# Expert slots worked on between pieces of later sequences' attention, with a slot table per sequence

## Chip, cores and metric

One core of a Trainium2 chip. The metric is the device time of one execution in microseconds (us); the kernel before takes 1216.33 us (median of 3 runs, 1215.55 to 1217.69).

## What is computed

```python
# q, k, v: (8 sequences, 8 heads, 576 positions, 64), float32
mask_plain = (rel >= 0) & (rel < 32)                             # heads 0-3
mask_dil   = (rel >= 0) & (rel < 128) & (rel % 4 == 0)           # heads 4-7
attn = softmax(where(mask, q @ k.T / 8, -1e9));  x = attn @ v    # x: (4608, 512)
expert_idx = argmax(x @ w_gate)                                  # 8 experts
y[tokens of e] = relu(x[tokens of e] @ w1[e]) @ w2[e]            # 512 -> 1024 -> 512
out = gate_w[:, None] * y                # gate_w: softmax weight of the chosen expert
```

Everything is float32. Which tokens an expert gets is known only when the router has run.

## The kernel before

**Attention.** The loop at L408 goes over 8 sequences b. A sequence has 8 units: type `ty` (0 sliding heads, 1 dilated heads), head pair `hl`, half of the queries `g`. `turn` (L173) turns q and k of two heads on PE, once for the two units of a pair. `front` (L220) is one unit's softmax: scores S on PE (L230), scale and mask on DVE (L242), a minimum on DVE (L252), six or eight exponentials on ACT that also sum (L255), `den` and `rec` on DVE (L263, L265), and the product with `rec` on POOL (L266). `back` (L271) turns the weights W on PE (L278), copies them out of PSUM as eT (L143), multiplies by v (X on PE, L292) and copies the result into xT (L145). `settle` lets a unit's `back` come two units after its `front`.

**Routing.** Behind each sequence's last unit `route` (L308) turns x back into rows (L314), computes logits (L324), each token's expert, gate and place among its expert's tokens (about 30 small DVE operations, L345 to L392, and the `rank` matmuls), and scatters the 576 rows into the experts' buckets in DRAM (six indirect DMAs on POOL, L113).

**Slots.** When all sequences are routed, a table (L435 to L505) gives each of 43 slots of 128 rows an expert, in the order of the experts, after eight scatters of blank rows that fill up the last slots of the experts. `fetch` (L512) loads a slot's rows x and, where its weight set still holds another expert's, w1 and w2 of 2 MB each; there are two sets, taken in turn. `slot` (L524) turns x (4 transposes), makes ph with w1 (32 matmuls, L537), takes the rectified h out of PSUM on ACT (first half, L545) and DVE (second half, L547), makes py with w2 (8 matmuls of 512 columns, L550), scales it on ACT (L552) and scatters it to the output on POOL (L555). One trace record is half of a matmul and a whole transpose.

**Order.** In this kernel the order of each engine's instructions is chosen by a scheduler, which moves instructions of different units past each other. The attention's pools are closed before the slots' pools are opened: PSUM is 3 buffers of two banks (`big`: scores, turned, weights) and 2 of one bank (`one`) in the attention. All loads of q, k, v, x and weights are issued from SP's queue, one behind the other.

Of the kernel before, what the change touches and what calls it, by code (L numbers as in the profile page):

```python
# [10 lines left out]
F32 = mybir.dt.float32  # L11
# [12 lines left out]
# Tokens go to the router in tiles of 96; six of them are one sequence.  # L24
TT, NT = 96, S // 96
# Each expert has a bucket of rows in DRAM that holds every token if need be; the experts' tokens
# are then worked on in slots of 128 rows, of which no routing needs more than NSLOT.
# [4 lines left out]
NOWHERE = 1.0e6  # L32


def _constants():
    """Masks, identity and index tables, side by side; all follow from the shapes."""
    i, j = np.arange(96)[:, None], np.arange(128)[None]

    def band(rel):
# [15 lines left out]
        "edge": np.tile(128 * np.arange(N // 128), (128, 1)),  # L55
        "row": p[:, None],
        "upto": np.tile((e[None] <= e[:, None]).reshape(1, -1), (128, 1)),
        "slot": np.tile(np.arange(NSLOT), (128, 1)),
    }
    at, k, cols = {}, 0, []  # L60
# [10 lines left out]
def kernel(  # L71
# [13 lines left out]

    cpool = ctx.enter_context(tc.tile_pool(name="cpool", bufs=1))
    cst = cpool.tile([128, packed.shape[1]], F32, name="cst")
# [7 lines left out]
    nc.vector.memset(blank[:, DM + 1 : ROW], NOWHERE)  # L95

# [7 lines left out]
    def wrote_bucket(i):  # L104
        """The writes to the buckets are to different rows: none waits for another."""
        i = getattr(i, "ins", i)
        tc.declare_no_dep(i, group="bucket", reason="no row is written twice")
        tc.add_to_no_dep_group("bucket", i)
        bucket_writes.append(i)

    def to_bucket(idx, rows):
        wrote_bucket(
            nc.gpsimd.indirect_dma_start(  # L113
                out=bucket,
                out_offset=bass.IndirectOffsetOnAxis(ap=idx, axis=0),
                in_=rows,
                in_offset=None,
                bounds_check=NROWS - 1,
                oob_is_err=False,
            )  # L120
        )

    # Unused slots read these rows.
    wrote_bucket(nc.sync.dma_start(bucket[E * CAP : NROWS], blank))

    # ---------------------------------------------------------------- attention
    attn = ExitStack()
    pool = attn.enter_context(tc.tile_pool(name="apool", bufs=2))
    big = attn.enter_context(tc.tile_pool(name="psbig", bufs=3, space=PSUM))
    one = attn.enter_context(tc.tile_pool(name="psone", bufs=2, space=PSUM))  # L130
# [16 lines left out]
    def load(b):  # L147
        """Heads 0-3 slide: q and k with a token in each partition of six tiles. Heads 4-7 are
        dilated: q and k with eight tokens in a row of a partition. v has the keys of each block of
        queries on the partitions."""  # L150
        t = {}
        for name, src in (("q", q), ("k", k)):
            x = t[name, 0] = pool.tile([TT, NT, 4, DH], F32, tag=name + "0", name=f"{name}0_{b}")
            for h in range(4):
                nc.sync.dma_start(x[:, :, h, :], src[b, h].rearrange("(t p) d -> p t d", p=TT))
        x = t["v", 0] = pool.tile([128, 4, NT, DH], F32, tag="v0", name=f"v0_{b}")
        nc.sync.dma_start(x[:, :, 0, :], v[b, 0:4, 0:128, :].rearrange("h p d -> p h d"))
        for h in range(4):
            a = v[b, h, 64:192, :]
            nc.sync.dma_start(  # L160
                x[:, h, 1:NT, :],
                bass.AP(a.tensor, a.offset, [[DH, 128], [TT * DH, NT - 1], [1, DH]]),
            )
        for name, src in (("q", q), ("k", k)):
            x = t[name, 1] = pool.tile([72, 4, 512], F32, tag=name + "1", name=f"{name}1_{b}")
            nc.sync.dma_start(x, src[b, 4:8].rearrange("h (p x) d -> p h (x d)", p=72))
        x = t["v", 1] = pool.tile([128, 4, 2, DIL * DH], F32, tag="v1", name=f"v1_{b}")
        for g in range(2):
            a = v[b, 4:8, 64 * g : 64 * g + 512, :]
            nc.sync.dma_start(x[:, :, g, :], a.rearrange("h (p r) d -> p h (r d)", r=DIL))  # L170
        return t

    def turn(t, ty, hl):  # L173
        """q and k of two heads, turned. Sliding: (head, dim) on the partitions, positions in order.
        Dilated: (residue's parity, dim) on the partitions, and head, the residue's other bit, and
        the residue's positions in order."""
        got = []
        for name in "qk":
            src = t[name, ty]
            dst = pool.tile([128, S], F32, tag=name + "T", name=name + "T", bufs=3)  # L180
            ps = bank2("turned")
            if ty == 0:
                for i in range(NT):
                    nc.tensor.transpose(
                        ps[:, i // 3, TT * (i % 3) : TT * (i % 3) + TT],
                        src[:, i, 2 * hl : 2 * hl + 2, :].rearrange("p h d -> p (h d)"),
                        ident[0:TT, 0:TT],
                    )
                evac(dst.rearrange("p (a t) -> p a t", a=2), ps[:, :, 0:288])
            else:  # L190
                for h in range(2):
                    for m in range(4):
                        nc.tensor.transpose(
                            ps[:, h, 72 * m : 72 * m + 72],
                            src[:, 2 * hl + h, 128 * m : 128 * m + 128],
                            ident[0:72, 0:72],
                        )
                    evac(
                        dst.rearrange("p (h m t a) -> p h a m t", h=2, m=2, a=2)[:, h],
                        ps[:, h, 0:288].rearrange("p (a m t) -> p a m t", a=2, m=2),  # L200
                    )
            got.append(dst)
        return got

    def blocks(ty, g):
        """The blocks of one half of the queries, by the half of the partitions that they are on:
        first query and first key in the turned q and k, head, and place among the half's."""
# [12 lines left out]
    def front(qT, kT, ty, g):  # L220
        """Softmax weights of two heads, queries on the partitions."""
# [19 lines left out]
        e = pool.tile([nq, 2, w], F32, tag=f"e{ty}", name="e", bufs=3)  # L241
# [29 lines left out]
    def back(ev, t, xT, ty, hl, g):  # L271
        """The weighted sum of v, with (head, dim) on the partitions and the tokens in order."""
        nq, bl = (96, 72)[ty], blocks(ty, g)
        nb = len(bl[0])
# [7 lines left out]
        evac(eT, tp[:, :, 0:288])  # L282
        xo = bank("xo")
        vt = t["v", ty]
# [23 lines left out]
    def route(b, xT):  # L308
        """Each token's expert, gate and row, and its x, gate and number to its expert's bucket."""
        rows = []  # L310
        for i in range(NT):
# [5 lines left out]
            row = pool.tile([TT, ROW], F32, tag="row", name="row", bufs=8)  # L317
            evac(row[:, 0:DM], ps[0:TT])
            rows.append(row)
        ps = bank("logits")  # L320
        lg = ps[0:TT, 0 : NT * E].rearrange("p (t e) -> p t e", e=E)
        for i in range(NT):
            for c in range(4):
# [6 lines left out]
                )  # L330
        shape = [TT, NT, E]
# [15 lines left out]
        # The first of equal logits has the largest of E - e.  # L347
# [5 lines left out]
        nc.vector.tensor_reduce(out=gate, in_=dl, axis=AX, op=OP.add)  # L353
        nc.vector.tensor_scalar(gate, gate, 1e-9, None, op0=OP.add)
        nc.vector.reciprocal(gate, gate)

        # How many tokens before this one have its expert: those of its tile, of the tiles before
        # it, and of the sequences before it.
# [4 lines left out]
        nc.vector.tensor_copy(counts, before[:, NT])  # L363
        ps = bank("rank")
# [14 lines left out]
        )  # L379
        pick, dest, idx = small("pick", NT, E), small("dest", NT), small("idx", NT, dt=I32)  # L380
# [9 lines left out]
        for i in range(NT):  # L390
# [8 lines left out]
            to_bucket(idx[:, i : i + 1], rows[i])  # L399

    waiting = []

    def settle(n):
        while len(waiting) > n:
            waiting.pop(0)()

    loaded = [load(0)]
    for b in range(B):  # L408
        t = loaded[b]
        xT = pool.tile([128, 4, S], F32, tag="xT", name=f"xT_{b}")  # L410
        for ty in range(2):
            for hl in range(2):
                qT, kT = turn(t, ty, hl)
                for g in range(2):
                    ev = front(qT, kT, ty, g)
                    settle(1)
                    waiting.append(
                        lambda ev=ev, t=t, xT=xT, ty=ty, hl=hl, g=g: back(ev, t, xT, ty, hl, g)
                    )
            if ty == 0 and b + 1 < B:  # L420
                loaded.append(load(b + 1))
# [179 lines left out]
```

## Time and profile before

| | us |
|---|---|
| median of 3 runs | 1216.33 |
| span of the profiled execution (first to last instruction) | 1191.1 |
| time of the runs less that span | 25.2 |
| PE busy in the span | 1036.2 (87%) |
| DVE, ACT, POOL busy | 328.2, 294.6, 201.8 |
| first score matmul | 13.54 |
| last scatter of routed rows begins | 513.6 |
| first ph matmul, last py matmul's end | 541.86, 1180.1 |

The profile gives busy time per engine, the clock that TensorE was granted (1.00 is full), and for stretches of the span the same numbers apart. A busy PE is a PE with a matmul in flight; at half clock it is as busy as at full clock and does less.

### The profile page before, as it was taken

Reading aid. Unit: us, or ns where it says so; the run is one execution under the profiler, and the core shown is the slowest. Engines: PE = TensorE matmul, PEld = TensorE weight load, DVE = VectorE, ACT = ScalarE, POOL = GpSimd, SP = SyncE. Lnnn points to the kernel's source line nnn. Section 1 sums busy time; section 2 is a strip of 40 time slices with the busy share of each in tenths; the row PEclk is TensorE's granted clock in tenths of the full one; section 3 lists DMA queues with packets and bytes.
Section 4 is the critical chain, followed back from the end, with each engine's and each line's share of the span. In section 5 each row is a group of like instructions: output and inputs, shape, how many; then the busy total and the mean of one; then the engine's idle time right before and its main releaser. Section 6 shows DMA issues by size and latency. Waiting matters only on the chain.

```text
span 1191.1 us, 17878 instructions
## 1 busy us (share of the span) xinstructions
PE 1036.2 (87%) x6910; PEld 796.0 (67%) x6910; DVE 328.2 (28%) x812; ACT 294.6 (25%) x1127; POOL 201.8 (17%) x167
## 2 busy tenths in 40 slices
PE   5797979788888888608999999999999999999996
PEld 4586857676767676506677777777777777777774
DVE  4555454545454645410100000101001011000000
ACT  3535354544445454300000000000000000000000
POOL 1314141424242424140000000000000000000000
PEclk9666676666667676658999999999999999999998
DMA  9934343434341101028172824545145451811100
GB/s 218 213 79 107 76 107 76 107 77 106 77 106 37 41 1 41 1 83 310 36 274 76 280 73 145 207 147 206 36 161 185 169 183 36 311 36 36 34 9 1
DMA packets 115684, 134.18 MB, mean 113 GB/s; under 512 B 67662, under 2 KB 75854, under 8 KB 115472
## 3 DMA queue, kind: packets, MB, share of 16 engines
q1 hardware_dynamic: 107776, 112.26, 32.3%
q0 software_dynamic: 7152, 19.71, 4.9%
q10 hardware_dynamic: 672, 1.07, 0.3%
q8 instruction: 55, 0.90, 0.3%
q14 instruction: 29, 0.24, 0.1%
HBM read 226.29 MB, written 23.11 MB: 209 GB/s over the span
## 4 chain that ended last, share of the span: by engine, by line
issue 51%; POOL 4%; POOLq 0%
POOL out_dram L555 3%; POOL bucket L113 0%; POOLq L555 0%; POOLq L597 0%
## 5 line engine op out<-in xcount | busy, mean ns | idle before, releaser
L537 PEld LDWEIGHTS ph<-xt,w 128*128 128x128 f32 x2752 | 314.9, 193 | 28.3 <-issue 14.6
L537 PE MATMUL ph<-xt,w 128*128 128x128 f32 x2752 | 319.3, 277 | 13.1 <-DVE xt L529 6.6
L550 PE MATMUL py<-w,h 128*128 128x512 f32 x688 | 302.4, 592 | 0.0
L550 PEld LDWEIGHTS py<-w,h 128*128 128x128 f32 x688 | 127.4, 190 | 144.0 <-issue 143.2
L255 ACT ACTIVATE e<-e,lo 72x128 f32<-72x128 f32 (+1 forms) x448 | 172.7, 388 | 33.2 <-DVE lo L252 21.2
L266 POOL TENSOR_TENSOR e<-e,rec 96x768 f32<-96x768 f32 (+1 forms) x64 | 107.6, 1681 | 330.3 <-DVE rec L265 303.9
L230 PE MATMUL scores<-kT,qT 64*72 64x128 f32 (+1 forms) x896 | 127.7, 417 | 35.8 <-ACT kT L145 35.8
L555 POOL DMA_INDIRECT out_dram<-y,to x43 | 41.8, 971 | 609.4 <-ACT y L552 609.4
L547 DVE TENSOR_SCALAR h<-ph 128x512 f32<-128x512 f32 x43 | 29.8, 692 | 411.4 <-issue 298.9
L552 ACT ACTIVATE y<-py,x 128x512 f32<-128x512 f32 x43 | 29.5, 687 | 421.2 <-PE py L550 421.2
L230 PEld LDWEIGHTS scores<-kT,qT 64*72 64x72 f32 (+1 forms) x896 | 92.1, 235 | 52.3 <-ACT kT L145 37.6
L278 PE MATMUL weights<-cst,e 72*128 72x72 f32 (+1 forms) x448 | 75.5, 329 | 24.9 <-ACT qT L145 17.6
L292 PE MATMUL xo<-eT,v 128*64 128x72 f32 (+1 forms) x896 | 82.1, 314 | 16.0 <-DVE idx L389 10.5
L242 DVE SCALAR_TENSOR_TENSOR e<-scores,cst 96x768 f32<-96x768 f32 (+1 forms) x64 | 69.4, 1084 | 84.3 <-PE scores L230 84.3
L292 PEld LDWEIGHTS xo<-eT,v 128*64 128x64 f32 x896 | 68.7, 195 | 28.7 <-issue 17.1
L278 PEld LDWEIGHTS weights<-cst,e 72*128 72x128 f32 (+1 forms) x448 | 56.5, 203 | 45.8 <-issue 30.4
L255 ACT ACTIVATION_READ_ACCUMULATOR e<-e,lo 72x1 f32 (+1 forms) x448 | 84.5, 189 | 0.0
L545 ACT ACTIVATE h<-ph 128x512 f32<-128x512 f32 x43 | 25.7, 597 | 200.1 <-PE ph L537 200.1
L145 ACT COPY xT<-xo 128x288 f32<-128x288 f32 x64 | 33.8, 528 | 164.5 <-PE xo L292 164.5
L252 DVE TENSOR_REDUCE lo<-e 96x6 f32<-96x768 f32 (+1 forms) x64 | 68.4, 1069 | 0.3
L529 DVE COPY xt<-xt 128x512 f32<-128x512 f32 x43 | 27.9, 687 | 122.5 <-PE xt L527 122.5
L143 DVE COPY eT<-weights 128x576 f32<-128x576 f32 x64 | 48.0, 749 | 16.3 <-PE weights L278 16.0
(82 smaller groups left out, 536.2 us busy)
## 6 DMA issues: line engine op xcount, KB each, us to landing
w<-in_moe_w_dram SPq DMA_DIRECT2D x86, 2048.0 KB
x<-bucket SPq DMA_DIRECT2D x43, 257.0 KB
v<-in_v_dram SPq DMA_DIRECT2D x16, 512.0 KB
v<-in_v_dram SPq DMA_DIRECT2D x32, 160.0 KB
q<-in_q_dram SPq DMA_DIRECT2D x32, 144.0 KB
k<-in_k_dram SPq DMA_DIRECT2D x32, 144.0 KB
q<-in_q_dram SPq DMA_DIRECT2D x8, 576.0 KB
k<-in_k_dram SPq DMA_DIRECT2D x8, 576.0 KB
```

What stands on the lines that cost most here:

```text
L143: nc.vector.tensor_copy(dst, src)
L145: nc.scalar.copy(dst, src)
L230: nc.tensor.matmul(sc[0:nq, r, 128 * n : 128 * n + 128], lhsT=qT[rows, q0 : q0 + nq], rhs=kT[rows, k0 : k0 + 128], start=True, stop=True,)
L242: nc.vector.scalar_tensor_tensor(out=e, in0=sc[0:nq, :, 0:w], scalar=-SCALE, in1=m.unsqueeze(1).broadcast_to([nq, 2, w]), op0=OP.mult, op1 ...
L252: nc.vector.tensor_reduce(out=lo, in_=ev, axis=AX, op=OP.min)
L255: nc.scalar.activation(out=ev[:, n], in_=ev[:, n], func=AF.Exp, bias=lo[:, n : n + 1], scale=-1.0, accum_out=den[:, n : n + 1],)
L266: nc.gpsimd.tensor_tensor(out=ev, in0=ev, in1=rec.unsqueeze(2).broadcast_to([nq, 2 * nb, 128]), op=OP.mult)
L278: nc.tensor.transpose(tp[:, r, nq * n : nq * n + nq], ev[:, nb * r + n], ident[0:nq, 0:nq])
L292: nc.tensor.matmul(xo[DH * h : DH * h + DH, nq * i : nq * i + nq], lhsT=vv, rhs=eT[:, r, nq * n : nq * n + nq], start=True, stop=True,)
L537: nc.tensor.matmul(ph[:, fi], lhsT=w1[:, c, 128 * f : 128 * f + 128], rhs=xt[:, c], start=c == 0, stop=c == 3,)
L550: nc.tensor.matmul(py, lhsT=h[:, f], rhs=w2[:, f], start=f == 0, stop=f == 7)
L555: i = nc.gpsimd.indirect_dma_start(out=out, out_offset=bass.IndirectOffsetOnAxis(ap=to, axis=0), in_=y, in_offset=None, bounds_check=N - 1 ...
```

## The change

Each expert's slots that are sure to be full need not wait for the last sequence. After b sequences at least (576 b - 8*127)/128 slots are full whatever the routing; the table of one such stage is made behind each sequence's routing from the second on, and its slots are worked on between pieces of the later sequences' attention. The stages end at slots 2, 6, 11, 15, 20, 24 and 43.

- `manual_schedule`: every engine runs its instructions in the order in which they are written, not in one that a scheduler chose.
- `attention` is a generator. It writes a unit's scores and softmax up to the product on POOL, then the W and, after the turns, the X of the unit two before, and gives a cost (1.2, 0.8, 0.7, 0.9) at each piece. q, k and v tiles have one buffer instead of two; PSUM is 2 two-bank buffers and 1 one-bank buffer for the attention, 2 for ph and 1 shared by py and the turned x.
- `moe` writes the slots as a generator too, 4 matmuls of ph (0.93) or 1 of py (0.88) a piece; the turned x of the next slot comes in the middle of a slot; a scatter is written in the next slot.
- The loop at the end writes, for each unit of attention cost, `rate` units of slots, where `rate` is what is left of the known slots over 42.
- The table has one more step: a stage takes the experts' free full slots in an order that is rotated by stage, and deals them to the two weight sets; the last stage is dealt in the same way. `fetch` gives x, w1 and w2 separately, as soon as the buffer's last reader is written.

```diff
+READY = [max(0, -(-(S * (b + 1) - E * 127) // 128)) for b in range(B)]
+READY[B - 1] = NSLOT
+LAG = 2
...
+    ctx.enter_context(tc.manual_schedule())
+    big = ctx.enter_context(tc.tile_pool(name="psbig", bufs=2, space=PSUM))
+    one = ctx.enter_context(tc.tile_pool(name="psone", bufs=1, space=PSUM))
+    psh = ctx.enter_context(tc.tile_pool(name="psh", bufs=2, space=PSUM))
+    psy = ctx.enter_context(tc.tile_pool(name="psy", bufs=1, space=PSUM))
...
+    def attention():
+        for i in range(len(units) + LAG):
+            if i < len(units):
+                evs[i] = front(qT["q"], qT["k"], ty, g)
+                yield 1.2, None
+            if i >= LAG:
+                eT = weights(evs.pop(i - LAG), ...)
+                yield 0.8, None
+            if i + 1 < len(units) and g == 1:
+                for n in "qk":
+                    qT[n] = turn(b2, ty2, hl2, n)
+                    yield 0.7, None
+            if i >= LAG:
+                summed(eT, b2, xTs[b2], ty2, hl2, g2)
+                yield 0.9, (b2, xTs.pop(b2)) if last else None
...
+    wanted = []
+    for j in range(NSLOT):
+        wanted += [(j, "x", 0, j - 2), (j, "w1", 0, j - 1), (j, "w2", 1, j - 1)]
...
+    def run_slots(limit):
+        while clock["owed"] > 0:
...
+            c = next(slots)
+            clock["moe"] += c
+            clock["all"] += c
+            clock["owed"] -= c
...
+                    clock["ready"].append((clock["all"] + 14.0, j1))
+                    left = SLOT * j1 - clock["moe"]
+                    clock["rate"] = left / 42.0
+    for cost, ended in attention():
+        clock["all"] += cost
+        clock["owed"] += cost * clock["rate"] / 2
+        run_slots(1e9)
+        if ended:
...
+            routing.append((ended[0], route(*ended, use)))
+        run_routing()
+        clock["owed"] += cost * clock["rate"] / 2
+        run_slots(1e9)
```

`front` itself is unchanged in text; `route` yields after each row tile, in the middle of the logits and before `rank`, and each yield is followed by attention and slot pieces.

## Prediction

> **What bounds it now.** I read the share of busy time and the granted clock over the span first, then stretches of the span, then the timelines of one attention unit and of one pair of slots, then the waits.
>
> From the profile page, the 40 slices of about 30 us:
>
> ```profile
> PE   5797979788888888608999999999999999999996
> PEclk9666676666667676658999999999999999999998
> ```
>
> Three stages: 17 slices of attention with PE at 0.7 to 0.9 and the clock near 0.67, a hole, and slots with PE full at clock 1.0. The same stages, as stretches (us; busy time and instructions of PE, PEld, DVE, ACT, POOL; clock; DMA share; GB/s):
>
> ```profile
> 212.00:274.00 62.00, 51.04 (x424) 42.54 (x424) 33.03 (x85) 30.55 (x135) 19.68 (x15) 0.67 0.38 88
> 264.00:268.00 4.00, 4.00 (x23) 3.13 (x23) 3.77 (x20) 1.61 (x9) 0.00 (x0) 0.50 0.00 0
> 493.00:541.90 48.90, 12.62 (x97) 10.24 (x96) 11.29 (x60) 2.66 (x5) 13.35 (x14) 0.57 0.29 98
> 541.90:558.00 16.10, 16.10 (x79) 12.75 (x80) 0.84 (x2) 0.60 (x1) 0.00 (x0) 0.82 1.03 393
> 558.00:1150.00 592.00, 583.84 (x3361) 424.57 (x3361) 57.34 (x121) 51.37 (x80) 38.86 (x40) 1.00 0.39 134
> ```
>
> A sequence costs 62 us, 51 of them with PE busy at 0.67; last routing, table and first loads leave PE idle for 36 of 48.9 us; 592 us of slots lose 8. So 11 us a sequence, 36 us of the hole, and the slow clock under the attention are all there is to win. Two slots on PE:
>
> ```profile
> 707.73 1.04 PE L527 MATMUL xt<-cst,x 128*128 128x128 f32 x8
> 709.12 7.41 PE L537 MATMUL ph<-xt,w 128*128 128x128 f32 x64 [0.35 <-DVE xt L529]
> 716.36 7.03 PE L550 MATMUL py<-w,h 128*128 128x512 f32 x16
> 723.23 7.31 PE L537 MATMUL ph<-xt,w 128*128 128x128 f32 x64
> 730.38 7.03 PE L550 MATMUL py<-w,h 128*128 128x512 f32 x16
> 737.25 1.04 PE L527 MATMUL xt<-cst,x 128*128 128x128 f32 x8
> ```
>
> From start to start two slots take 29.52 us, 14.76 each: 7.22 ph (0.226 a matmul), 6.87 py (0.859), 0.52 of transposes, the rest a wait that the change removes. So 14.61 is a slot.
>
> **The written order.** The built order of the changed kernel has on DVE, for every unit, L242, L252, den, rec, and only then the eT copy of the unit two before. den needs the last exponential, and PE's X needs eT, and the next S stands behind X. So a unit has a chain in which nothing overlaps. Its links, from a stretch where nothing else is in the way:
>
> ```profile
> 13.54 2.88 PE L230 MATMUL scores<-kT,qT 64*96 64x128 f32 x24 [0.73 <-ACT kT L145]
> ...
> 15.18 0.95 DVE L242 SCALAR_TENSOR_TENSOR e<-scores,cst 96x768 f32<-96x768 f32 x1 [4.06 <-PE scores L230]
> ...
> 16.17 0.95 DVE L252 TENSOR_REDUCE lo<-e 96x6 f32<-96x768 f32 x1
> ...
> 17.15 0.40 ACT L255 ACTIVATE e<-e,lo 96x128 f32<-96x128 f32 x1 [3.67 <-DVE lo L252]
> ...
> 19.60 0.17 DVE L263 TENSOR_SCALAR den<-den 96x6 f32<-96x6 f32 x1
> 19.80 0.19 DVE L265 RECIPROCAL rec<-den 96x6 f32<-96x6 f32 x1
> ```
>
> From 15.18 to rec's end at 19.99 is 4.81; with 0.08 ahead, the eT copy (0.76) and 0.08 of hops, C = 5.73 us from S to X for a sliding unit. A dilated one has 1.22 and 1.20 on DVE and eight exponentials 0.385 apart: C = 7.08. Now the scheduler puts other units' work into that gap; DVE waits little for it (62 us from 212; total, times, longest):
>
> ```profile
> DVE den L263 <- ACT e L255: 6.9, 5, 2.7
> ```
>
> After the change it waits 2.4 or 3.2 us in each of 8 units.
>
> **Sequences 0 to 2, without slots.** A unit costs S + C + X, plus one turn (its second PSUM buffer comes free only with eT) where g is 1. At half clock, start to start: S 1.53 or 1.90, X 1.13 or 1.65, turn 1.0 or 0.9. Units: 8.4 and 9.4 sliding, 10.6 and 11.5 dilated, 10.1 and 11.0 where the type changes. Sequence 0: the first two, which have no X, 12.0, then 8.4 + 9.4 + 10.1 + 11.0 + 10.6 + 11.5 = 73. Sequences 1 and 2 carry routing: row transposes behind X 1.1 in two units; the unit with logits has 9.9 instead of C, then 3.4 of waits for `rank` and the row operations: 88.6. Sequence 2 also has a table, 24 small DVE operations between rec and eT; rows of the present table (0.09 to 0.2 each, two of 0.45) give 4.3. From 13.5 the first S of sequence 3 starts at 268 if all is at half clock, 257 if a third is at full as now. I take 265; three sequences cost now 186.
>
> **Sequences 3 to 7, with slots.** Counting PE's built order, 19.2 of the 43 slots lie ahead of the last S. A unit costs S + max(C, what PE has between S and X) + X + what PE has behind X. At full clock: S 0.80 or 1.04, W 0.55 or 0.58, X 0.60 or 0.90, turn 0.52, row tile 0.50, logits 0.196 a matmul. Example, sequence 4's last two units: (1) 12 ph 2.71 + W 0.58 + 2 py 1.72 = 5.01, under C: 1.04 + 7.08 + 0.90 + 3 py 2.58 = 11.60, PE idle for 2.1. (2) 3 py, W, 8 ph, turn, 8 ph, turn, transposes, 4 ph = 9.22: 1.04 + 9.22 + 0.90 + 8 ph 1.80 = 12.97, not idle. So every other unit hides C, the others lose 0 to 3 us. The sequences: 82.9, 95.7, 99.4, 100.0 and 87.5 (seven units) = 465.5. On top, per sequence: table 4.3; `rank` and row operations 2.5; one PSUM bank for row tiles and X, so that two copies behind ACT or DVE stand ahead of X, 2.5; the slots' DVE copies (0.69) ahead of eT, 2.3: 11.6, five times 58. Sequence 3 has slots in 37 of its 83 us only; 8 for half clock there.
>
> **Tail.** PE's order from the last S: 364, nearly all slots, with the last routing between them. From `tot` to the first slot of the last stage are 34 us of slots. Needed: six row scatters and eight blank ones at 1.22 and 1.28 a step, 17.6, about 4 to land, then x and w1: 2 MB at 393 GB/s is 5.3; about 30. So the hole goes; 4 for waits. Behind the last py 11, as now (1180.1 to 1191.1).
>
> **Loads.** Run on the reference's inputs, the table has 16 loads of a weight pair before and 30 after: 59 MB more. A pair is 4.19 MB, 10.7 us at 393 GB/s. Each is asked for 22 us of slots ahead of use, and between attention a slot lasts some 25 us. A sequence has 4.3 slots, at most 46 us of weights and about 23 of other DMA (0.38 of 62) in 110: hidden, cost 0; if the cover fails, up to 10.7 a load. The constants are 0.3 MB more on ACT's queue; they land at 6.6, with q needed at 9.1: 0, else 1. POOL's and SP's issues keep their number apart from loads; a scatter of 0.97 ahead of a product has two units of slack.
>
> **Sum.** 265 + 465.5 + 58 + 8 + 364 + 4 + 11 = 1175.5 against 1191.1, 15.6 less. The runs' median lies 25.2 above the span: **1200.7 us**. The change wins 282 us of slots under attention and 40 of the hole, and pays them back in longer attention. The unknowns: the added waits, 58, lie between 10 (all but the table's under slots) and 130 (each of 19 slots held 4 us more by h or y behind the exponentials); the clock.
>
> The row at 264 has PE busy all of 4 us at 0.50, while slots get 1.00 within 16 us (0.82 there); so attention's matmuls alone do not raise the clock, slots do, and mixed ones are some 60% slots. I take full clock there. The Trainium skill, "TensorE: Matmul & The Clock Gate", "Why this matters for your kernels", says to avoid idle gaps over about 3 us. By that, sequences 0 to 2 (gaps of 5 us in each unit) stay at half throughout, 3 us more than I take, and the mixed ones stay full; its rule that 4 us of continuous work gives full clock is not what the row at 264 shows.
>
> **Rivals.**
> - *Waits stack up* (slower): DVE and ACT, held by den and the exponentials, also hold the slots' h, turned x and y, so PE idles in pieces that I count as full. For it: each stands behind them in the built order. Against: most are read half a slot later. At 130 instead of 58: **1273**; it decides from 16 us of extra idle.
> - *The clock drops* in mixed sequences to 0.8 on average: 92 us of PE work a sequence becomes 115, some of it in idle time: 20 in each of 4.4: **1289**. For it: attention's 0.67; against: slots' 1.00.
> - *Weight loads are late*, 2 us for each of 20 loads between attention: **1241**. For: single SP queue; against: 22 us of lead.
> - *Waits hide* (faster): 10 instead of 58, and 257 for the first stage: **1145**.
> - That slots do not move is excluded by the built order.
>
> **Chances.** Sum as worked, 1180 to 1225: 0.50. Waits stack up: 0.15. Clock: 0.10. Loads: 0.07. Waits hide: 0.18. The range 1143 to 1272 leaves out half of the clock and stacking cases and part of the last. A measurement tells 0.2% (2.4 us) from no change. Faster: 0.37 of the first and the last, 0.55; same 0.05; slower 0.40.
>
> **What would show it.** Each step: about 85 us between first scores of sequences 0 to 2; waits of den for the exponentials over 150 us in total; about 110 us per mixed sequence with PE over 85% and clock over 0.95; the last stage's first slot without a gap; ph's waits for weights near 0. Wrong if PE idles over 20 us in a mixed sequence or its clock is under 0.9.

## Result and the profile after

The changed kernel takes 1252.84 us (median of 4 runs, 1251.94 to 1253.76), the kernel before beside it 1215.94 (4 runs, 1214.11 to 1217.69): a ratio of 1.030, 95% interval 1.028 to 1.032. It is slower by 37 us, where 1200.7 was forecast; the profiled execution has a span of 1251.5 us at a mean clock of 0.859.

The slices of the changed kernel's page, about 31 us each:

```profile
PE   3546656546768896998789699977979999999996
...
PEclk8566556567689968999889999989988999999999
```

The hole ahead of the slots is gone and the clock is up from a third of the span on, as the change means it. But the attention now reaches to slice 28, with PE at 0.3 to 0.6 for the first nine. Stretches of the changed kernel: sequences 0 and 2, 3 to 7 (the last without its last unit), tail (the columns as before):

```profile
14.80:89.00 74.20, 36.97 (x288) 30.03 (x286) 27.09 (x44) 27.98 (x124) 13.43 (x8) 0.59 0.31 73
182.00:279.00 97.00, 53.35 (x410) 45.30 (x406) 39.43 (x107) 30.54 (x129) 19.00 (x14) 0.59 0.46 146
279.00:402.00 123.00, 89.37 (x650) 68.81 (x650) 43.66 (x115) 34.84 (x136) 21.21 (x16) 0.79 0.40 125
402.00:529.00 127.00, 105.99 (x750) 79.73 (x750) 46.13 (x119) 36.25 (x138) 23.05 (x18) 0.85 0.59 192
529.00:649.00 120.00, 103.67 (x772) 76.87 (x771) 45.68 (x120) 35.93 (x138) 23.00 (x18) 0.94 0.47 151
649.00:765.00 116.00, 100.18 (x790) 76.83 (x790) 45.29 (x120) 37.15 (x140) 24.04 (x19) 0.97 0.68 220
765.00:867.00 102.00, 89.42 (x698) 67.76 (x697) 40.88 (x113) 31.79 (x120) 20.11 (x16) 0.97 0.51 171
867.00:1251.00 384.00, 361.10 (x2151) 266.71 (x2146) 52.05 (x147) 37.88 (x71) 39.72 (x40) 0.98 0.49 166
```

The mixed sequences take 102 to 127 us and leave PE idle for 13 to 34 us in each. The two waits that name the cause, on VectorE and on TensorE (total, times, longest):

```profile
DVE den L303 <- ACT e L295: 182.7, 62, 3.6
```

```profile
PE xo L337 <- DVE eT L178: 60.5, 12, 10.8
PE turned L234 <- ACT qT L180: 32.5, 16, 4.4
```

`den` waited five times, 6.9 us in all, in the old stretch of 62 us; it now waits for the exponentials in 62 of the 64 units, 2.9 us each. TensorE's 60.5 us are only the waits that end with `eT` itself. One unit of sequence 1 in the changed kernel's timeline (start, duration, instruction, and idle time before it with its releaser):

```profile
88.02 1.19 PE L270 MATMUL scores<-kT,qT 64*96 64x128 f32 x12
...
89.14 0.72 PE L317 MATMUL weights<-cst,e 72*128 72x72 f32 x8
89.26 0.95 DVE L282 SCALAR_TENSOR_TENSOR e<-scores,cst 96x768 f32<-96x768 f32 x1 [2.07 <-PE scores L270]
90.25 0.95 DVE L292 TENSOR_REDUCE lo<-e 96x6 f32<-96x768 f32 x1
...
93.75 0.17 DVE L303 TENSOR_SCALAR den<-den 96x6 f32<-96x6 f32 x1 [2.56 <-ACT e L295]
93.96 0.19 DVE L305 RECIPROCAL rec<-den 96x6 f32<-96x6 f32 x1
94.06 0.71 DVE L178 COPY eT<-weights 128x576 f32<-128x576 f32 x1
...
94.92 1.73 PE L337 MATMUL xo<-eT,v 128*64 128x72 f32 x16 [5.06 <-DVE eT L178]
96.59 1.60 PE L270 MATMUL scores<-kT,qT 64*96 64x128 f32 x12
```

Read it from the bottom. The product X at 94.92 waits 5.06 us for the copy `eT` of a unit two before, whose input, the turned weights, was ready at 89.9. The copy starts at once behind `rec`; `rec` and `den` belong to the present unit and stand ahead of it on VectorE; `den` waits for the exponentials. From the mask step to X are 5.66 us, the chain C of 5.73. The Trainium skill, "PSUM — Partial Sum Buffer", "Engine vs sequencer instructions", says that VectorE's queue is strictly first in, first out; the copy that has its data and does not start for 4 us agrees with it.

### The profile page after: what moved, and what is told of

It reads as the page before. It is cut to its first block, busy times and chain, and to the rows that moved or that the text cites. A ratio compares the mean times of both kernels' runs of the same rounds, so it can differ in the third digit from the quotient of the medians.

```text
span 1251.5 us, 18337 instructions
## 1 busy us (share of the span) xinstructions
PE 998.9 (80%) x6922; PEld 762.0 (61%) x6922; DVE 376.2 (30%) x973; ACT 305.5 (24%) x1127; POOL 202.9 (16%) x167
## 4 chain that ended last, share of the span: by engine, by line
PE 64%; DVE 15%; ACT 14%; issue 6%; SPq 1%; DMA 0%; ACTq 0%; POOLq 0%; DVEq 0%
PE ph L684 21%; PE py L708 21%; ACT e L295 12%; PE scores L270 6%; PE xo L337 6%; DVE e L282 5%; DVE lo L292 5%; PE logits L407 4%; PE turned L234 2%; PE xrow L396 2%; PE xt L664 1%; PE turned L225 1%; DVE eT L178 1%; ACT qT L180 1%; ACT kT L180 1%
## 5 line engine op out<-in xcount | busy, mean ns | idle before, releaser
L684 PE MATMUL ph<-xt,w 128*128 128x128 f32 x2752 | 354.0, 284 | 14.5 <-issue 9.5
L684 PEld LDWEIGHTS ph<-xt,w 128*128 128x128 f32 x2752 | 335.8, 198 | 35.4 <-issue 27.4
L708 PE MATMUL py<-w,h 128*128 128x512 f32 x688 | 335.6, 622 | 2.3 <-ACT qT L180 1.8
L337 PE MATMUL xo<-eT,v 128*64 128x72 f32 (+1 forms) x896 | 75.2, 297 | 125.4 <-DVE eT L178 60.5
L270 PE MATMUL scores<-kT,qT 64*72 64x128 f32 (+1 forms) x896 | 82.9, 336 | 4.1 <-DVE qT L178 3.4
L270 PEld LDWEIGHTS scores<-kT,qT 64*72 64x72 f32 (+1 forms) x896 | 65.9, 188 | 29.2 <-issue 20.0
L303 DVE TENSOR_SCALAR den<-den 96x6 f32<-96x6 f32 (+1 forms) x64 | 10.7, 168 | 189.4 <-ACT e L295 182.7
L156 POOL DMA_INDIRECT bucket<-row,idx x48 | 44.6, 929 | 131.9 <-DVE row L478 119.7
L317 PEld LDWEIGHTS weights<-cst,e 72*128 72x128 f32 (+1 forms) x448 | 44.7, 159 | 14.8 <-issue 14.6
L317 PE MATMUL weights<-cst,e 72*128 72x72 f32 (+1 forms) x448 | 50.5, 260 | 0.0
```

The source lines that it names most:

```text
L156: nc.gpsimd.indirect_dma_start(out=bucket, out_offset=bass.IndirectOffsetOnAxis(ap=idx, axis=0), in_=rows, in_offset=None, bounds_check=NR ...
L270: nc.tensor.matmul(sc[0:nq, r, 128 * n : 128 * n + 128], lhsT=qT[rows, q0 : q0 + nq], rhs=kT[rows, k0 : k0 + 128], start=True, stop=True,)
L317: nc.tensor.transpose(tp[:, r, nq * n : nq * n + nq], ev[:, nb * r + n], ident[0:nq, 0:nq])
L337: nc.tensor.matmul(xo[DH * h : DH * h + DH, nq * i : nq * i + nq], lhsT=vv, rhs=eT[:, r, nq * n : nq * n + nq], start=True, stop=True,)
L684: nc.tensor.matmul(ph[:, fi], lhsT=w1[:, c, 128 * f : 128 * f + 128], rhs=xt[:, c], start=c == 0, stop=c == 3,)
L708: nc.tensor.matmul(py, lhsT=h[:, f], rhs=w2[:, f], start=f == 0, stop=f == 7)
```

## Experiments

Each set of runs has its own runs of the kernel before. These stood at 1216.2 us in the first set and at 1194.4, 1193.3 and 1193.3 in the second to fourth; what sets this level stays open (below). The first two sets ran on one chip and the other two on two others, so the chip alone does not set it. Times are compared within a set or between the last three.

### First set: the place of the sums, the order, the mixing, the loads

**The sums closed late.** `den`, `rec` and POOL's product are written behind the X of the unit two before.

```diff
-        nc.vector.tensor_scalar(den, den, 1e-9, None, op0=OP.add)
-        ... rec, product
+        def finish():
+            ... den, rec, product
+        finishing.append(finish)
...
                 summed(eT, b2, xTs[b2], ty2, hl2, g2)
+                while finishing:
+                    finishing.pop(0)()
```

> The changed kernel with one edit: den, rec and the product of a unit are written behind the X of the unit two before, so eT's copy on DVE no longer stands behind the exponentials. Theory A (the written order's chain S, DVE, exponentials, den, eT, X holds PE): sequences 0 to 2 fall from 75, 93 and 98 us to 65 to 75 each, PE's waits of X for eT nearly vanish, mixed sequences lose some 10 us each: about 1130 to 1170 us against 1253. Rival B (the slow clock under sparse matmuls sets the time, waits only move elsewhere): less than 25 us gained.

Measured: 1145.3 us, ratio 0.944 (0.941 to 0.948). Repeated in the fourth set, beside that set's runs:

> The late closing of the sums once more, to be compared with its other place (1120.8 us, just behind the copy of the turned weights) in runs where the kernel before is at 1194 us. The first measurement, 1145.3 us, had that kernel at 1216 us. If the level of the set of runs explains the difference between the two places: 1118 to 1130 us. If the later place is the worse one: 1136 to 1148 us.

Measured: 1119.85 us, ratio 0.939 (0.937 to 0.940). Three instructions a unit, moved by a few lines, turn 3% slower into 6% faster. The move is worth 107.5 us within the first set, and 123 us, 1.9 in each of 64 units, for the repeated run against the changed kernel in the third set (1242.84). VectorE's wait in the repeated run:

```profile
DVE den L307 <- ACT e L297: 40.3, 24, 2.7
```

40 us are left of 182.7. TensorE's X waits 20.4 us for `eT` there, where it was 60.5.

**Order alone.** The kernel before with the written order as its only change.

```diff
+    ctx.enter_context(tc.manual_schedule())
```

> The kernel before with one edit: every engine runs in written order; slots stay behind the attention. Theory A: the same chain appears in all 8 sequences, 62 us become 85 to 95 each, so about 1216 + 200 = 1420 us; den waits for the exponentials about 180 us in all. Rival B (it is the mixing and the smaller PSUM pools that cost): under 1260 us.

Measured: 1562.46 us (one run), more than either side gave. A sequence takes 105 us instead of 61. This kernel still has the buffers of the kernel before, and its X waits for `eT` in 63 of the 64 units, 293.2 us in all: the chain comes with the order and not with the smaller pools.

**No mixing.** The changed kernel with the slots' pace set to zero: no slot before the attention's end.

```diff
-                    clock["rate"] = left / 42.0
+                    clock["rate"] = 0.0
```

> The changed kernel with the slots' rate under attention set to 0, so that all slots are worked on behind the last attention unit. Theory A: all 8 sequences as long as the first three were (98 with routing and table): 279 + 5 x 98 = 769, then 10 + 43 x 14.61 + 11: about 1418 us, so the mixing itself wins some 165 us and the written order loses more. Rival C (mixing hides little, since slots and attention hold one another up): under 1320 us.

Measured: 1461.38 us (one run). With the two before it, the change comes apart into three parts: the written order +346 (1216 to 1562), the rest without mixing −101 (to 1461; 30 of it ahead of the last scores, 71 behind them, where the hole closes), the mixing −209 (to 1253). The mixing does what it was made for; it is less than the price of the order.

**No reloads.** Weights are loaded for the first two slots alone; the loads for the other slots are left out.

```diff
-... value_load(newi[:, n : n + 1], min_val=0, max_val=1) > 0
+... value_load(newi[:, n : n + 1], min_val=0, max_val=1) > 1
```

> The changed kernel, which loads no expert's weights after the first two sets (later slots use the wrong weights, so the loads are left out of the work). If the 30 loads are hidden as I priced them: within 5 us of the changed kernel, but for the stall of some 10 us ahead of the last stage, if that is a late load. Rival D (loads late between attention): 30 to 50 us faster, and the gain lies in sequences 3 to 7.

Measured: 1252.89 us. The 30 loads of weight pairs cost nothing, as forecast.

### Second set: three waits apart, and the kernel before again

**Late sums, and turned copies on VectorE.** All copies of turned q and k (before in turns on ACT and VectorE); the copies of dilated tiles are changed in the same way:

```diff
-            evac(dst.rearrange("p (a t) -> p a t", a=2), ps[:, :, 0:288])
+            nc.vector.tensor_copy(dst.rearrange("p (a t) -> p a t", a=2), ps[:, :, 0:288])
...
```

> Both copies of each turned q and k tile go to VectorE, on top of the late closing of the softmax sums (1145.3 us, with 33.0 us of TensorE waiting for ScalarE's copies of qT in 16 waits). Theory (ScalarE copies qT behind the exponentials of the unit before, and TensorE's second half of the same tile waits for it): most of the 33 us goes, 1112 to 1130 us, and the wait of the turned tiles for ScalarE is gone from the trace. Rival (VectorE is as late with the copy, because it stands behind the score step of the unit, and has more to do): the wait changes its engine and 1138 to 1155 us is measured.

Measured: 1101.58 us. Against the repeated late sums (1119.85) that is 18.3 us, not the 33 that waited for ScalarE; the 43.7 against the first set holds that set's level.

**Table later.** The changed kernel with the slot table of each stage but the last one piece later.

```diff
             if b2 == b:
                 yield
+                if s + 1 < len(STAGES):
+                    yield
                 tables(s, bank)
```

> The changed kernel with one edit: the slot table of every stage but the last is written one piece of attention later. Theory (the table's VectorE steps stand between the sums of one unit and the turned weights of the unit that TensorE waits for, 7.3 to 8.9 us of wait in each of six stages, and TensorE's clock is halved for some us after each): 4 to 6 us less in each of six stages, 1217 to 1232 us. Rival (VectorE has to do the table somewhere and every place in the written order is on the same loop): 1245 to 1257 us.

Measured: 1217.54 us; the changed kernel in the third set, with the kernel before within 0.1%, has 1242.84. So 25 us, 4.2 in each of six stages. One table in the changed kernel's timeline, the py records ahead of it and then from its last VectorE step on:

```profile
346.23 1.91 PE L708 MATMUL py<-w,h 128*128 128x512 f32 x4
...
356.24 0.74 DVE L178 COPY eT<-weights 128x576 f32<-128x576 f32 x1
356.91 0.13 DVE L714 CAST to<-x 128x1 int32<-128x1 f32 x1
357.04 1.23 PE L337 MATMUL xo<-eT,v 128*64 128x96 f32 x12 [8.90 <-DVE to L714]
358.19 3.72 PE L708 MATMUL py<-w,h 128*128 128x512 f32 x4
```

The table's steps run from 350.70 to 356.3 between `rec` and `eT`, so this unit's X waits 8.90 us; and the four py records behind it take 3.72 us, 0.93 each, where the four ahead of the wait took 0.48 each (0.43 in the kernel before at full clock). The idle time costs twice: itself, and then at half clock. The Trainium skill, "TensorE: Matmul & The Clock Gate", "Why this matters for your kernels", names idle gaps over about 3 us as what drops the clock; here half rate followed a gap of 8.90.

**All three.** Late sums, turned copies on VectorE, later table.

> Late closing of the sums, turned copies on VectorE and the later table together. Theory (three separate waits in one loop, each with its own price): the gains add, 1090 to 1115 us. Rival (one limit lies behind all three, as the clock or TensorE's own order): not under 1125 us, and no faster than the better of the two edits by more than 0.5%.

Measured: 1073.2 us, ratio 0.898 (0.897 to 0.900). The gains add: the table takes another 28.4.

**The kernel before, profiled again.**

> The kernel before, unchanged, profiled a second time. If the execution profiled first (span 1191.1 us at a mean clock of 0.839) was an unusual one, this one has a span of 1211 to 1217 us at a clock of 0.81 to 0.825, its time is 1.3 to 2.2 us over the span, and the difference lies in the attention stage (first 540 us), where the first profile has clocks of 0.59 to 0.72. If profiling itself makes the execution shorter, the span is 1189 to 1194 us again.

Measured: 1196.47 us with a span of 1194.6 at a clock of 0.831. So an execution with a span near 1191 is no oddity and not due to being profiled: the seven runs of this kernel beside it are at 1191.8 to 1195.2, with clocks of 0.839 to 0.845, and all of the first set at 1214.1 to 1218.7, with 0.815 to 0.823. In both, time less span is under 2 us.

### Third set: what stands behind the wait

**The changed kernel again.**

> The changed kernel once more, beside runs of the kernel before. That kernel has been measured at 1216 us in one set of runs and at 1194 us in another, with granted clocks of 0.82 and 0.84; the changed one only once, at 1252.84 us. If the level belongs to the set of runs, the changed kernel moves by the same 1.8% with it (1230 us where before is at 1194); if only the kernel before has two levels, the changed one is at 1250 to 1256 us in any case, and its ratio is 1.03 or 1.05 by the level of the other.

Measured: 1242.84 us, ratio 1.042 (1.039 to 1.044). It moves with the level, by 0.8%, where the kernel before moves by 1.9%; so both theories fall, and the loss is 3.0 or 4.2% by the set. Its two profiled executions differ by 12.4 us (1251.5 and 1239.1), and all of that lies behind the last scores: from there to the end are 384.9 us in the first and 371.5 in this one.

**Turned copies on VectorE alone**, with the sums where the change has them.

> Both copies of the turned q and k go to VectorE, but the sums are closed where the change has them, between score step and turned weights. Theory (the wait of VectorE for ScalarE's exponentials is ahead of these copies too, so they come no sooner on VectorE than on ScalarE): a gain under 15 us, 1238 to 1256 us, though the same edit took off 43.7 us where the sums are closed late. Rival (the copies wait for nothing but their engine's length of work, and the edit has its own price): 1205 to 1225 us.

Measured: 1274.75 us, 32 slower than the changed kernel beside it, where the same edit wins 18 with the sums closed late. Both expectations fall: the theory was right that the copies come no sooner on VectorE, but it forecast a small gain, and a loss came. Waits of TensorE in it:

```profile
PE turned L234 <- DVE qT L239: 46.2, 16, 5.5
...
PE turned L225 <- DVE eT L178: 26.1, 7, 5.4
```

The same two waits in the changed kernel of the same set:

```profile
PE turned L234 <- ACT qT L180: 33.2, 16, 4.4
...
PE turned L225 <- ACT qT L180: 21.1, 7, 4.4
```

The waits change their engine and grow, by 13 and 5 of the 32 us; where the rest comes from was not traced. VectorE is not the idle engine that its busy share (30%) says, but one that stands at `den`.

**The sums closed just behind `eT`**, so still ahead of the turned copies that are VectorE's.

```diff
                 eT = weights(evs.pop(i - LAG), ...)
+                while finishing:
+                    finishing.pop(0)()
```

> The closing of the sums (add, reciprocal, product) is moved only past the copy of the turned weights, so it still stands ahead of the turned q and k and of the copy of the sum over v on VectorE. Theory (what costs is that the copy of the turned weights, which TensorE needs next, stands behind the wait for the exponentials): most of the 107 us of the later place, 1140 to 1175 us. Rival (anything behind that wait on VectorE costs as much, the turned tiles too): 1190 to 1240 us.

Measured: 1120.83 us, as much as the later place (1119.85 in the fourth set). So what the late place wins is had by `eT` ahead of `den` alone; the expectation's numbers were built on the first set's level.

**Late sums without mixing.**

> The sums closed late, and no slot worked on before the attention has ended (the pace of the slots is set to zero; the same work in another order). With the early place the mixing was worth 1461 - 1253 = 208 us. Theory (the late place repairs a loop that costs in every unit, with or without slots: about 1.7 us in each of 64): 1330 to 1375 us, so that mixing is worth 190 to 230 us here too. Rival (mixed units lose the most by the early place, unmixed ones little): 1400 to 1440 us.

Measured: 1307.48 us (one run), under both ranges. Mixing is worth 188 us here against 209 with the early sums, and the early place costs 154 without slots (2.4 a unit; sets of different levels) against 123 with them. The wait costs in every unit; slots cover a part of it at most.

### Fourth set: what the mixed sequences are made of

**Turns ahead of copies.** Of a dilated tile, all eight turns are written before its two copies.

```diff
             for h in range(2):
                 for m in range(4):
                     nc.tensor.transpose(...)
+            for h in range(2):
                 evac(...)
```

> The changed kernel with one edit: of a dilated tile all eight turns are written ahead of its two copies, where before the second four turns waited for the copy of the first four (33.2 us of TensorE's wait for ScalarE's copies of qT in 16 waits, 8.0 us for those of kT). Theory (this wait is a term of the mixed sequences that the prediction left out): 15 to 33 us less than the 1242.8 us of the last set of runs, 1208 to 1228 us. Rival (the score steps behind wait for the same copies, so the wait only moves): 1236 to 1250 us.

Measured: 1213.75 us, 29 less than the changed kernel. How the copy holds the turns, in the changed kernel's timeline:

```profile
367.07 0.42 PE L234 MATMUL turned<-cst,q 72*128 72x72 f32 x4
...
368.74 0.58 ACT L694 ACTIVATE h<-ph 128x512 f32<-128x512 f32 x1
...
369.21 0.40 ACT L180 COPY qT<-turned 128x288 f32<-128x288 f32 x1
369.66 0.47 PE L234 MATMUL turned<-cst,q 72*128 72x72 f32 x4 [2.17 <-ACT qT L180]
```

The first four turns end at 367.5; their copy waits on ScalarE behind eight exponentials and a slot's `h` until 369.21; the other four turns, which go to another bank, wait for the copy. No datum is missing: they are written behind it, and the tile is shared. With all turns ahead, this wait for ScalarE (32.5 us in the changed kernel) is gone from the trace, and the dilated turns wait 18.9 us for `eT` instead.

**Both of these.**

> Turns ahead of copies, and the slot table one piece later (25 us by itself between sets of runs that agree on the kernel before to 0.1%). Theory (two separate terms of the 55 us that the mixed sequences take over the forecast): 1183 to 1205 us. Rival (they overlap in the same loops): 1208 to 1225 us.

Measured: 1182.1 us, ratio 0.990 (0.988 to 0.992). 60.7 less than the changed kernel, where the two alone give 29.1 and 25.3. So the change is 1% faster than the kernel before with the sums still in the early place, once these two waits are gone. The stretch from the logits of sequence 3 to those of sequence 4, in the changed kernel (third set):

```profile
457.00:581.00 124.00, 108.09 (x810) 83.35 (x809) 46.77 (x120) 36.49 (x139) 24.05 (x19) 0.90 0.60 201
```

And in this one:

```profile
431.00:540.00 109.00, 101.27 (x812) 79.53 (x812) 45.58 (x121) 37.31 (x140) 24.03 (x19) 0.97 0.74 248
```

The same work (810 and 812 records) takes 15 us less: 8 less idle, 7 less busy at the higher clock. Here the low clock follows from the waits. It is not so everywhere: from first score to first score, the clock of the first mixed sequence (number 3) is 0.79 in the changed kernel and 0.78 with both edits; of the next two it goes from 0.86 and 0.89 to 0.97.

**The three edits, with turns ahead of copies.**

> The three edits (1073.2 us) with the turns of a dilated tile ahead of its copies, which are on VectorE here. If the second half still waits for the first one's copy there: 1055 to 1070 us. If late closing has made room for these copies: 1070 to 1077 us.

Measured: 1027.69 us, ratio 0.861 (0.859 to 0.862): 45.5 less than the three edits, more than the 24.3 us that the turned tiles still waited for their copies there (15.4 and 8.9), and outside both ranges. What the other 21 us are was not tried; the clock is 0.936 against 0.907. Its page:

```profile
PE   3878787789999999999999999999999999999995
...
PEclk9996565788999999999999999999999999999998
```

From the tenth slice on PE is full. What is left lies ahead of it, where at most two slots are known to be full.

The 9s of the first three slices of PEclk are not full speed: six records of the turned weights W take 1.22 us there up to 46 us, as they do at half clock; at full rate they take 0.66. The profile shows 1.00 from the start until the clock first falls, at 72.7 us here and at 45 us in the three edits, though TensorE works at half rate until about 68 and 41 us. About half of the step from 0.907 to 0.936 is only that, and mean clocks of whole runs are to be read with it in mind.

The time of the first routing step behind the logits, in us, shows where each edit wins:

| kernel | sequence 0 | 2 | 4 | 7 | span |
|---|---|---|---|---|---|
| changed (third set) | 131.9 | 335.0 | 581.5 | 914.7 | 1239.1 |
| table later | 133.9 | 331.1 | 559.3 | 888.7 | 1215.4 |
| turns ahead of copies | 129.4 | 328.5 | 560.5 | 885.6 | 1210.3 |
| both | 131.8 | 324.4 | 540.3 | 854.7 | 1181.5 |
| sums late (fourth set) | 110.2 | 273.0 | 487.9 | 792.0 | 1116.8 |
| three edits, turns ahead | 98.1 | 238.0 | 425.6 | 704.1 | 1031.3 |

Behind the last logits all need 324 to 327 us: the tail is slots and does not change.

## Why the prediction was wrong

The forecast span was 1175.5, the first profiled one is 1251.5: 76 us more, of which 14 lie in sequences 0 to 2, 56 in 3 to 7 and 6 in the tail.

- **The chain of the written order** was right: C = 5.73 against 5.66, waits of `den` 182.7 us where over 150 was asked for. Sequences 0 to 2 were to take 73, 88.6 and 92.9; from first score to first score they take 74.8, 93.1 and 98.0. The first S of sequence 3 came at 279.1, for 265. (The "186" that three sequences cost in the kernel before is three times 62; from first score to first score they take 167.0, since the first takes 44.6.) 3 of the 14 are the clock: 268 was worked out for half and 257 for a third at full, and 265 taken; with 0.59 it stayed near half. 3 lie between two executions of the changed kernel (275.8 in the third set), and 4 are what the two edits of the fourth set take off by that score (271.7). The other 4 stay open.
- **The clock of sequences 0 to 2** was nearer to half than taken. The Trainium skill's rule on gaps ("TensorE: Matmul & The Clock Gate", "Why this matters for your kernels") gave half clock there, and the 0.59 is near it. The rule does not give the clock everywhere: in sequence 0 of the last kernel of the fourth set, TensorE falls from full to half rate between 90 and 93 us (eight turned records take 0.67 us at 89.67 and 1.20 at 93.15), and no gap is over 1.6 us in the 10 us before. The prediction's own reading, that attention's matmuls alone do not raise the clock, came from one row of 4 us and is wrong: in the kernel before, in sequence 2 and so without slots, the six records of W take 1.22 us at 141.90 and 0.71 at 159.88.
- **The term that failed** is the added waits of the mixed sequences, "five times 58", that is 11.6 a sequence and 58 in all. Forecast with 8 for the clock, first score to first score: 102.5, 107.3, 111.0, 111.6 and 99.1; measured 122.8, 127.2, 120.2, 115.9 and 101.3. The table was priced with the length of its own steps, 4.3 (5.6 here). What was not priced is that X waits through it behind a chain already at its end, and then runs at half clock; nor the dilated turns' wait for their own copies, which has no term at all. Taking both away wins 60.7 us, 55 of them from sequence 3's first score to the last scores (591.7 before, 536.9 after), against 56 too many; 531.5 was forecast for this stretch.
- **Full clock in mixed sequences** was wrong for the first two (0.79 and 0.85) and near for the others (0.94 to 0.97). The rival "clock drops" named it as a cause; in the second and third mixed sequence it is a consequence, since it rises to 0.97 when the two waits go. In the first it stays at 0.78; for that one the prediction had 8 us of half clock.
- **"Waits stack up"** was the likeliest of the slower rivals and its mechanism is what happened: VectorE and ScalarE, held by `den` and the exponentials, hold other work. But the prediction placed them at the slots' h, y and turned x; the work that was held was the attention's own `eT` and turned tiles, and the table ahead of `eT`. Its 0.15 was too little: the argument against it, "most are read half a slot later", holds for the slots' tiles and not for the attention's, which TensorE needs next.
- **Loads** at no cost: right (1252.89 without them). **The hole** goes: right. **The tail**: 379 forecast, 384.9 measured; between 928 and 940 single ph records stand up to 2.44 us apart with no wait shown, some 9.5 us in all, beside the last stage's scatters. This stall, 8.2 to 9.5 us, is in all four profiles of the first set that have the stages (the changed kernel, late sums, no mixing, no reloads) and in none of the three later sets, which have the same scatters; there the changed kernel's tail is 371.5. So most of the 10 us by which the changed kernel moves between sets lie in it, and the tail itself was forecast 7 too long. What the records wait for stays open; not for weights, since the stall is there without reloads too.
- **25.2 us outside the span** was wrong and hid a third of the error. Time less span is 2 us. The profiled execution of before belonged to the level of 1194, the runs to that of 1216. At one level the forecast is some 1177 us against 1194, and the measured one 1243: 65 too low. No profile at the level of 1216 was taken, so where those 22 us lie in the kernel before is open; its mean clock over the whole run is lower there (0.82 against 0.84).

## What to carry to other kernels

When an order is written out by hand, look on every engine for what stands behind an instruction that waits for another engine, and put the copies that TensorE needs next ahead of it: here three small instructions behind a copy instead of ahead of it were worth 107 to 123 us. Price added work on such a chain with the idle time and the clock of the engine at its end, not with its own length, and look for the same wait inside each helper that writes two halves in turn. Before a span and a set of runs are put into one sum, see whether time less span is the same in other runs.

## What the runs showed of the hardware

- After a wait of 8.90 us TensorE worked at half rate for 3.72 us (0.93 a py record, 0.48 ahead of the wait).
- Attention's matmuls alone reach full rate at times (six records of W in 0.71 us at 159.88 in the kernel before, 1.22 at 141.90), and can fall to half without a long gap: eight turned records took 0.67 us at 89.67 and 1.20 at 93.15 in the last kernel, with no gap over 1.6 us in the 10 us before.
- The profile's clock stood at 1.00 for the first 20 to 73 us of the changed kernels, though the first records were already at half rate (W 1.22 us for six records).
- The kernel before, unchanged, stood at 1214 to 1219 us in the first runs and at 1190 to 1197 in three later sets, without values between. It moved by 1.9%, the changed kernel by 0.8%, the late sums by 2.2%. In the changed kernel, most of it is one stall of TensorE with no releaser shown (9.5 us in the first set, none in the third).
- An engine that is busy 30% of the span can be the one that is late: the turned copies moved from ScalarE to VectorE cost 32 us with `den` ahead of them and won 18 without.
